# A fused attention and MLP kernel: the first loads on two queues, MLP columns and the weight transposes reordered in the opening

## The chip, the cores and the metric

One core of a Trainium2 chip runs the whole program. The metric is the time of one execution on the device, in microseconds (us). Engines are named as the profile names them: PE (matrix engine), PEld (its weight loads), DVE (VectorE), ACT (ScalarE), POOL (GpSimd), SP (the engine that issues most of the transfers here).

## The reference

The input is 2,048 tokens of 640 elements. The reference normalises them (LayerNorm without scale), puts the result through a linear attention of 32 heads with a softmax feature map and through a SwiGLU MLP of 1,536 columns, and adds both to the input. Everything is bf16. Cut to what matters here:

```python
xn = layernorm(x)
qkv = xn @ wqkv                                # 32 heads of 20
pk = einsum("bhsd,hdf->bhsf", k, w_phi)        # likewise pq from q
phi_k = concat([softmax(pk), softmax(-pk)])
o  = (phi_q @ (phi_k^T v)) / (phi_q . sum(phi_k) + 1e-6)
h  = silu(xn @ w1) * (xn @ w3)
out = x + o @ wo + h @ w2
```

## The kernel before

The kernel brings x in as sixteen tiles of 128 tokens. It needs xn transposed (`xnT`: channels on the partitions). Tiles 0 to 3 are transposed on PE; tiles 4 to 15 by DMA transposes, issued on the SP queue. Because `w_phi` is block diagonal, the kernel multiplies it into wk and wq once ("fold": `Wkp = wk @ blockdiag(w_phi)`), and for that it loads wk transposed (`wqkT`, five DMA transposes).

A list scheduler in the kernel file runs at build time. It models the engines and fixes a static order of instructions for each; waits follow from dependencies. All matmuls are issued by one helper and all vector work by another, so the profile shows one line number for each (L572 and L580 before, L619 and L627 after); the tiles' names tell them apart.

The loads, in the order of their priority:

```python
load_x(0, 1, lv)
load_x(1, 2, lv - 1)
load_wv(0, 2, lv - 2, "SP")
load_x(2, 3, lv - 3)
load_wv(2, 5, 2e9, "ACT")
load_x(3, 4, lv - 4)
load(phi_s[:], phi_t, 2e9 - 1e3, "ACT")
for e in range(DC):
    load_wT(1, e, lv - 9 - e)                  # wk, transposed by DMA
load_w13(0, 256, lv - 16)                      # MLP columns 0-255 of w1 and w3
load_x(4, 8, 1.9e6, "ACT")                     # held back by the model to 9 us
load_w13(256, 512, lv - 20)
load_x(8, 12, lv - 21)
load_w13(512, 1024, lv - 22)
load_x(12, 16, lv - 23)
load_w13(1024, 1536, lv - 24)
...
for t in range(4, T, 2):
    ln_stats(t, 2, 1e5 - t)
    ln_apply(t, 2e5 - t)
    ln_apply(t + 1, 2e5 - t)
    turn(xnT[:, :, t * 128:(t + 1) * 128], x_tok[:, t, :], lv)      # DMA transpose, on SP
    turn(xnT[:, :, t * 128 + 128:(t + 2) * 128], x_tok[:, t + 1, :], lv)
```

V of the first tiles does not wait for the whole LayerNorm: x is centred (by ACT and DVE, `CENTRED`), transposed and multiplied, and the scale is applied when V leaves PSUM. The full normalisation of the same tile, which K and the MLP need, is done apart; `POOLED` puts it on POOL for tiles 0 and 1:

```python
CENTRED = {0: "ACT", 1: "ACT", 2: "DVE", 3: "DVE"}
POOLED = (0, 1)
...
def ln_apply(t, level):
    o, m, s, z = x_tok[:, t, :], mv[:, t, 0:1], mv[:, t, 4:5], mv[:, t, 6:7]
    ways = [w_op("DVE", "tensor_scalar", (o, o, m, s, ALU.subtract, ALU.mult), 0.35, 0.44)]
    if t in POOLED:
        ways = [w_op("POOL", "tensor_scalar", (o, o, m, s, ALU.subtract, ALU.mult), 1.25, 1.3)]
    ...
```

V of tile 4 reads `xnT` and `wv`:

```python
def proj(t, w):
    for i in range(DC):
        for q in range(2):
            mm(q, lambda k, q=q: bank(k + q, 320), xnT[:, i, t * 128:(t + 1) * 128],
               w[:, i, 320 * q:320 * q + 320], i == 0, i == DC - 1)

def v_tile(t, level):
    P.begin(2, level, stream="V").name = f"V{t}"
    proj(t, wv)
    ...
```

One MLP column (`M0.0` is the first column of the first 512 tokens) is ten matmuls of 128x512, which PE issues every 0.216 us (215 or 216 ns between starts in the trace of before): about 2.16 us. The sums below use 2.155. These columns are what the scheduler puts wherever PE would otherwise wait.

The softmax here doesn't subtract the row's maximum and nothing guards it: scores larger than these inputs give would overflow.

## Time and profile before

| before | |
|---|---|
| time | 276.63 us, median of 4 runs, 276.57 to 276.64 |
| span in the profile | 274.9 us |
| first V matmul | 6.85 us |
| fold of wk starts | 15.78 us |
| first MLP column (M0.0) starts | 23.26 us |
| V of tile 4 starts | 33.84 us |
| `xnT` of tile 4 has landed | 29.68 us, so 4.16 us ahead of its use |

The first part of the profile's page has the busy time of each engine with its share of the span and its instructions; the second has the same in 40 slices of 6.9 us, in tenths. Before:

```profile
PE 266.7 (97%) x2078; PEld 158.9 (58%) x2097; DVE 183.1 (67%) x319; ACT 102.6 (37%) x187; POOL 65.7 (24%) x103
...
PE   6799999999999999999999999999999999999996
```

PE is the limit, and full from the third slice on. Only the opening has anything to give. What held it there is in the chain of waits (start, duration in us, what), followed back from what ended last in the first 41 us; its first microseconds, before:

```profile
0.81 2.27 DMA x_tok<-in_A_x_dram
...
5.74 2.53 POOL x_tok L580
...
9.36 2.53 POOL x_tok L580
...
11.93 0.45 PE PS L787 x5
```

Two normalisations of 2.53 us on POOL stand in line ahead of PE's transposes at 11.93 us. The scheduler's model had priced each at 1.25 to 1.3 us (the `ways` of `POOLED` above), half of what it took. The timeline of PE gives the order of its work (start, us from first start to last end, what, count; in brackets an idle time and what ended it). Before:

```profile
11.93 0.45 PE L787 MATMUL PS<-ident,x_tok 128*128 128x128 bf16 x5 [1.64 <-POOL x_tok L580]
...
15.78 1.87 PE L572 MATMUL PS<-BDc,wqkT 128*128 128x140 bf16 x30
17.60 5.61 PE L572 MATMUL PS<-Wkp,xnT 128*128 128x320 bf16 x40
23.26 10.74 PE L572 MATMUL PS<-xnT,w_s 128*128 128x512 bf16 x49
33.84 1.52 PE L572 MATMUL PS<-wv,xnT 128*128 128x320 bf16 x10
```

The rows after the POOL wait are the fold (`BDc,wqkT`), K of tiles 0 to 3 (`Wkp,xnT`) and five MLP columns (`xnT,w_s`; 49 of the 50 matmuls have a record). V of tile 4 (`wv,xnT`) follows at 33.84 us.

### The profile page before, as it was taken

The page shows a single profiled execution, that of the slowest core. Times are in us where ns is not written, and L with a number is a line of the kernel's source. Part 1 is how long each engine was busy: PE and PEld are TensorE (multiplying, and loading weights), DVE is VectorE, ACT ScalarE, POOL GpSimd, SP SyncE. Part 2 cuts the span into 40 slices and gives each one's busy share as a digit, 9 for nine tenths or more (in the row PEclk, how much of TensorE's full clock was granted, in tenths as well). Part 3 has the DMA queues.
Part 4 walks back from the last instruction along what each step waited for, and adds up shares of the span by engine and source line. Part 5 has one row for each costly group of instructions (what it writes and reads, how often), then busy time and mean ns, then how long its engine had stood idle before and what let it go on. Part 6 is the DMA issues. An engine that isn't in the chain of part 4 may idle for free.

```text
span 274.9 us, 5053 instructions
## 1 busy us (share of the span) xinstructions
PE 266.7 (97%) x2078; PEld 158.9 (58%) x2097; DVE 183.1 (67%) x319; ACT 102.6 (37%) x187; POOL 65.7 (24%) x103
## 2 busy tenths in 40 slices
PE   6799999999999999999999999999999999999996
PEld 3575477656654447544444445677777774444774
DVE  4698989999957433678978978577661215666112
ACT  6379377564553451256673382010000002222000
POOL 5923556999997000000000000000000000000000
PEclk9999999999999999999999999999999999999999
DMA  7999997910000000803211111243332222000001
GB/s 216 237 317 347 195 132 129 187 67 0 2 0 2 0 0 2 284 6 27 47 26 24 38 36 24 75 99 95 97 96 75 72 72 74 0 0 0 26 24 48
DMA packets 41255, 21.98 MB, mean 80 GB/s; under 512 B 27024, under 2 KB 41232, under 8 KB 41232
## 3 DMA queue, kind: packets, MB, share of 16 engines
q1 hardware_dynamic: 39648, 20.49, 31.2%
q10 hardware_dynamic: 1584, 1.17, 1.5%
q8 instruction: 16, 0.26, 0.4%
q14 instruction: 7, 0.06, 0.1%
HBM read 12.81 MB, written 2.62 MB: 56 GB/s over the span
## 4 chain that ended last, share of the span: by engine, by line
PE 91%; POOL 3%; ACT 2%; DVE 1%; issue 1%; DMA 1%
PE PS L572 91%; POOL x_tok L580 2%; ACT EqT L580 2%; DMA x_tok<-in_A_x_dram 1%; POOL mv L580 1%; PE PS L787 0%; DVE bst L580 0%; DVE hT L580 0%; DVE den_s L580 0%; DVE xres L580 0%; ACT e_s L580 0%; DVE xc L580 0%; PE PS L757 0%; DVE t L580 0%; DVE pr_s L580 0%
## 5 line engine op out<-in xcount | busy, mean ns | idle before, releaser
L572 PE MATMUL PS<-xnT,w_s 128*128 128x512 bf16 x465 | 105.6, 379 | 1.4 <-issue 0.5
L572 PEld LDWEIGHTS PS<-xnT,w_s 128*128 128x128 bf16 x480 | 46.4, 98 | 54.5 <-DVE hT L580 0.8
L572 PE MATMUL PS<-w_s,hT 128*128 128x320 bf16 x384 | 55.0, 299 | 0.0
L580 ACT ACTIVATE th<-PS 128x512 f32<-128x512 f32 x48 | 28.7, 599 | 66.0 <-PE PS L572 66.0
L580 DVE SCALAR_TENSOR_TENSOR t<-th,PS 128x512 bf16<-128x512 f32 x48 | 32.6, 679 | 24.0 <-ACT th L580 23.9
L572 PEld LDWEIGHTS PS<-w_s,hT 128*128 128x128 bf16 x384 | 37.1, 98 | 14.9
L580 DVE TENSOR_TENSOR xres<-PS,xres 128x640 bf16<-128x640 f32 (+1 forms) x17 | 13.4, 786 | 41.2 <-PE PS L572 41.2
L580 POOL TENSOR_TENSOR ekt<-ekt,rS 128x640 bf16<-128x640 bf16 x32 | 39.6, 1275 | 1.5 <-DVE rS L580 1.5
L580 DVE SCALAR_TENSOR_TENSOR hT<-t,PS 128x512 bf16<-128x512 bf16 x48 | 32.5, 677 | 1.3 <-PE PS L572 0.3
L580 ACT ACTIVATE EqT<-PS 128x512 bf16<-128x512 f32 x40 | 21.9, 594 | 12.6 <-PE PS L572 12.6
L580 DVE TENSOR_REDUCE S<-ekt 128x64 f32<-128x1280 bf16 x16 | 22.9, 1458 | 3.4 <-ACT ekt L580 3.4
L572 PE MATMUL PS<-wo_s,oT 128*128 128x320 bf16 x160 | 24.5, 299 | 0.0
L580 DVE TENSOR_TENSOR prod<-PS,g_s 128x1280 bf16<-128x1280 f32 x16 | 23.8, 1490 | 0.5
L580 ACT ACTIVATE ekt<-PS 128x640 bf16<-128x640 f32 x32 | 20.8, 701 | 8.6 <-PE PS L572 8.4
L572 PE MATMUL PS<-Wkp,xnT 128*128 128x320 bf16 x160 | 23.9, 299 | 0.0
L572 PE MATMUL PS<-xnT,Wqp 128*128 128x512 bf16 x96 | 23.1, 380 | 0.3 <-issue 0.2
L580 ACT ACTIVATE e_s<-PS 128x64 f32<-128x64 f32 x32 | 9.1, 284 | 37.6 <-PE PS L572 37.1
L572 PEld LDWEIGHTS PS<-wo_s,oT 128*128 128x128 bf16 x160 | 15.7, 98 | 6.1
L572 PEld LDWEIGHTS PS<-Wkp,xnT 128*128 128x128 bf16 x160 | 15.5, 98 | 6.0
L572 PE MATMUL PS<-wv,xnT 128*128 128x320 bf16 x120 | 18.3, 299 | 0.0
L580 DVE BATCH_NORM_STATS2 bst<-x_tok 128x6 f32<-128x320 bf16 x32 | 14.3, 469 | 3.0 <-DMA x_tok<-in_A_x_dram 3.0
L572 PEld LDWEIGHTS PS<-xnT,Wqp 128*128 128x128 bf16 x100 | 9.3, 98 | 10.8
(68 smaller groups left out, 172.1 us busy)
## 6 DMA issues: line engine op xcount, KB each, us to landing
w_s<-in_B_w_dram SPq DMA_DIRECT2D x4, 640.0 KB, 9.2
xres<-in_A_x_dram SPq DMA_DIRECT2D x16, 160.0 KB, 2.2
out_dram<-xres SPq DMA_DIRECT2D x15, 160.0 KB, 1.8
w_s<-in_B_w_dram SPq DMA_DIRECT2D x1, 1920.0 KB, 9.2
w_s<-in_B_w_dram SPq DMA_DIRECT2D x4, 320.0 KB, 5.5
x_tok<-in_A_x_dram SPq DMA_DIRECT2D x2, 640.0 KB, 8.4
wo_s<-in_A_wo_dram SPq DMA_DIRECT2D x1, 800.0 KB, 4.9
x_tok<-in_A_x_dram SPq DMA_DIRECT2D x4, 160.0 KB, 4.0
```

Of the source, the lines that this page charges most:

```text
L572: return nc.tensor.matmul(o(u.k), l, r, start=start, stop=stop, skip_group_check=shared)
L580: return getattr(e, name)(*[at(a, u) for a in args], **{k: at(v, u) for k, v in kw.items()})
```

## The change

Its intent is to start PE's real work earlier and to keep it fed. The first 1.5 MB alternate between the SP and the ACT queue; the normalisation of tiles 0 and 1 goes from POOL to DVE, and the mean of tile 2 for its centring from DVE to ACT; V of tiles 0 and 1 becomes one unit; w1 and w3 columns 0 to 383 are loaded early and three MLP columns stand ahead of the fold; and to let those loads through, the wk transposes wait until `w_phi` has landed. All later loads wait until the last wk transpose has landed (`d.raw.add(o)`). The scheduler's model of the DMA queues is rewritten and a new random seed chosen, with the random choices going on to 175 us of the model instead of 25; the first four loads of `xres` (x again, for the sum at the end) are held back to 60 us of the model. The core of the diff:

```diff
-CENTRED = {0: "ACT", 1: "ACT", 2: "DVE", 3: "DVE"}
-POOLED = (0, 1)
-SEED = 0
+CENTRED = {0: "ACT", 1: "ACT", 2: "ACT", 3: "DVE"}
+POOLED = ()
+SEED = 65
... (the model of the queues in the scheduler left out)
+    def v_pair(t, level):          # V of tiles t and t + 1 as one unit of four banks
+        P.begin(4, level, stream="V").name = f"V{t}+"
+        for a, b, u in ((0, 3, 0), (0, 3, 1), (3, DC, 0), (3, DC, 1)):
... (matmuls and copies as in v_first)
     load_x(0, 1, lv)
-    load_x(1, 2, lv - 1)
-    load_wv(0, 2, lv - 2, "SP")
-    load_x(2, 3, lv - 3)
-    load_wv(2, 5, 2e9, "ACT")
-    load_x(3, 4, lv - 4)
-    load(phi_s[:], phi_t, 2e9 - 1e3, "ACT")
+    on_act(1.3, load_x, 1, 2)
+    load_wv(0, 2, lv - 1)
+    on_act(1.75, load_wv, 2, 3)
+    load_x(2, 3, lv - 2)
+    on_act(2.2, load_wv, 3, 4)
+    load_wv(4, 5, lv - 3)
+    on_act(2.65, load_x, 3, 4)
+    load_w13(0, 384, lv - 4)
+    load(phi_s[:], phi_t, lv - 5)
+    first = [P.all[-1]]
     for e in range(DC):
-        load_wT(1, e, lv - 9 - e)
-    load_w13(0, 256, lv - 16)
+        o = load_wT(1, e, lv - 9 - e, first)
+    load_x(4, 8, lv - 19, "SP", [o])
     n = len(P.all)
-    load_x(4, 8, 1.9e6, "ACT")
-    late(n, 9.0)
-    load_w13(256, 512, lv - 20)
+    load_w13(384, 768, lv - 20)
     load_x(8, 12, lv - 21)
-    load_w13(512, 1024, lv - 22)
+    load_w13(768, 1152, lv - 22)
     load_x(12, 16, lv - 23)
-    load_w13(1024, 1536, lv - 24)
+    load_w13(1152, 1536, lv - 24)
     for e in range(DC):
         load_wT(0, e, lv - 30 - e)
+    for d in P.all[n:]:
+        d.raw.add(o)
...
-    for t in range(4):
+    v_pair(0, 6e4)
+    for t in range(2, 4):
         (v_first if t in CENTRED else v_tile)(t, 6e4 - 10 * t)
...
-    P.schedule({"PE": 1.25, "ACT": 2.1, "DVE": 0.93, "POOL": 0.8, "SP": 0.81}, filler, 12.0, SEED, 25.0)
+    P.schedule({"PE": 1.25, "ACT": 1.12, "DVE": 0.93, "POOL": 0.8, "SP": 0.81}, filler, 12.0, SEED, 175.0)
```

More of the change, by code (lines that the diff above doesn't have):

```diff
@@ L36 @@
     __slots__ = ("ways", "eng", "emit", "raw", "war", "bankd", "succ", "unit", "ismm", "start", "end", "inc", "sem",
-                 "clock", "idx", "part", "level", "off", "done", "nbytes", "busy", "left", "name", "deps", "gates", "early", "extra")
+                 "clock", "idx", "part", "level", "off", "done", "nbytes", "busy", "left", "name", "deps", "gates", "early", "extra",
+                 "begin", "each")
     def __init__(self, ways):
@@ L160, in op, with dma @@
         return self.add(o, writes, reads, level, after)
-    def dma(self, eng, emit, writes, reads, nbytes, busy=0.45, level=0.0, after=()):
+    def dma(self, eng, emit, writes, reads, pieces, each, busy=0.45, level=0.0, after=()):
         o = _Op({eng: (emit, busy, 0.0)})
-        o.nbytes = nbytes
+        o.nbytes, o.each = pieces, each
         return self.add(o, writes, reads, level, after)
@@ L206, in schedule @@
         bus = 0.0
+        issue = {"ACT": start["ACT"]}
+        queues = {"SP": [], "ACT": []}
         mode = "full"
@@ L215, in schedule, with transfer @@
                     ready[e].append(o)
+        def transfer(now):
+            nonlocal bus
+            at = dict.fromkeys(queues, 0)
+            left = {q: [o.nbytes for o in v] for q, v in queues.items()}
+            t = 0.0
+            bus = 0.0
+            while True:
+                go, wake = [], 1e9
+                for q, v in queues.items():
+                    if at[q] < len(v):
+                        o = v[at[q]]
+                        if o.begin <= t + 1e-9:
+                            go.append(q)
+                        else:
+                            wake = min(wake, o.begin)
+                if not go:
+                    if wake > 1e8:
+                        break
+                    t = wake
+                    continue
+                turn = sum(queues[q][at[q]].each for q in go)
+                steps = min(left[q][at[q]] for q in go)
+                if wake < t + steps * turn:
+                    steps = (wake - t) / turn
+                t += steps * turn
+                for q in go:
+                    left[q][at[q]] -= steps
+                    if left[q][at[q]] < 1e-6:
+                        o = queues[q][at[q]]
+                        e = t + 1.3 + o.extra
+                        if e > now:
+                            o.end = e
+                        at[q] += 1
+                bus = t
+            for q, v in queues.items():
+                while len(v) > 1 and v[0].end < now - 5.0 and v[1].begin < now - 5.0:
+                    v.pop(0)
         def commit(o, e, t):
-            nonlocal bus, pool_prev
+            nonlocal pool_prev
             o.eng = e
@@ L221, in commit @@
             o.start = t
-            free[e] = t + o.busy
+            free[e] = max(free[e], t + o.busy)
+            if e == "ACT":
+                issue[e] = t + (o.busy if o.nbytes else 0.06)
             if o.nbytes:
-                bus = max(bus, t + 0.6) + o.nbytes / 1e3
-                o.end = bus + 1.2 + o.extra
+                o.begin, o.end = t + 0.6, 1e9
+                queues[e].append(o)
+                transfer(t)
             else:
@@ L326, in schedule @@
                     continue
-                ts = [(max(free[e], op_time(o, e)), o) for o in ready[e]]
+                ts = [(max(issue[e] if o.nbytes and e == "ACT" else free[e], op_time(o, e)), o) for o in ready[e]]
                 t = min(x[0] for x in ts)
@@ L446, in emit @@
         return lists
-CENTRED = {0: "ACT", 1: "ACT", 2: "DVE", 3: "DVE"}
-POOLED = (0, 1)
-SEED = 0
+CENTRED = {0: "ACT", 1: "ACT", 2: "ACT", 3: "DVE"}
+POOLED = ()
+TURNED = ()
+SEED = 65
 TRIPLES = ((0, 3, 0, 60), (3, 3, 60, 60), (6, 3, 120, 60), (9, 3, 180, 60), (12, 3, 240, 60), (13, 3, 300, 20))
@@ L633, in bass_parallel_sum__linear_kernel_hedgehog__glu_gated_swiglu__prompt_kernel, with pieces @@
     queue = {"SP": nc.sync, "ACT": nc.scalar}
-    def bus(o, elem):
+    def pieces(o, elem):
         n = 1
@@ L638, in bus, with turn @@
             n *= s
-        return n * 2 / elem / 16 * max(18.0, 10 + 0.0352 * elem) + 100.0
+        return n * 2 / elem / 16, max(18.5, 12 + 0.04 * elem) / 1e3
     def load(o, i, level=0.0, eng="SP", after=()):
-        return P.dma(eng, lambda: queue[eng].dma_start(o, i), sb(o), sb(i), bus(o, 2 * o.shape[-1]), 0.45, level,
+        return P.dma(eng, lambda: queue[eng].dma_start(o, i), sb(o), sb(i), *pieces(o, 2 * o.shape[-1]), 0.45, level,
                      after)
-    def turn(o, i, level=0.0, dram=False):
-        d = P.dma("SP", lambda: nc.sync.dma_start_transpose(o, i), sb(o), sb(i), bus(o, 256),
-                  1.31, level)
+    def turn(o, i, level=0.0, dram=False, after=()):
+        d = P.dma("SP", lambda: nc.sync.dma_start_transpose(o, i), sb(o), sb(i), *pieces(o, 256),
+                  1.31, level, after)
         d.extra = 1.0 if dram else 0.2
@@ L658, in bass_parallel_sum__linear_kernel_hedgehog__glu_gated_swiglu__prompt_kernel, with load_x, load_w1, load_w3 @@
     w3_t = B_w3.rearrange("(c p) f -> p c f", p=128)
-    def load_x(a, b, level, eng="SP"):
-        load(x_tok[:, a:b, :], x_t[:, a:b, :], level, eng)
-    def load_w13(a, b, level, eng="SP"):
-        load(w1_s[:, :, a:b], w1_t[:, :, a:b], level, eng)
-        load(w3_s[:, :, a:b], w3_t[:, :, a:b], level, eng)
-    def load_wT(which, e, level):
-        turn(wqkT[:, which * DC + e:which * DC + e + 1, :],
-             A_wqkv[:, which * D + 128 * e:which * D + 128 * e + 128], level, True)
+    def load_x(a, b, level, eng="SP", after=()):
+        return load(x_tok[:, a:b, :], x_t[:, a:b, :], level, eng, after)
+    def load_w1(a, b, level, eng="SP"):
+        return load(w1_s[:, :, a:b], w1_t[:, :, a:b], level, eng)
+    def load_w3(a, b, level, eng="SP"):
+        return load(w3_s[:, :, a:b], w3_t[:, :, a:b], level, eng)
+    def load_w13(a, b, level, eng="SP"):
+        load_w1(a, b, level, eng)
+        load_w3(a, b, level, eng)
+    def load_wT(which, e, level, after=()):
+        return turn(wqkT[:, which * DC + e:which * DC + e + 1, :],
+                    A_wqkv[:, which * D + 128 * e:which * D + 128 * e + 128], level, True, after)
     zeroed = []
     def consts():
+        memset("DVE", warm[:], 0.0, 19)
         memset("DVE", zero[:], 0.0, 9)
         zeroed.append(P.all[-1])
-        memset("DVE", warm[:], 0.0, 9)
         add([w_act(warm[:], warm[:], ACT.Exp, 8)], [warm[:]], [warm[:]], None, 3e9)
@@ L730, in ln_apply @@
         if t in POOLED:
-            ways = [w_op("POOL", "tensor_scalar", (o, o, m, s, ALU.subtract, ALU.mult), 1.25, 1.3)]
+            ways = [w_op("POOL", "tensor_scalar", (o, o, m, s, ALU.subtract, ALU.mult), 2.5, 2.55)]
         if t >= 4:
@@ L777, in v_first, with src @@
             [v2[:, t, 0:672]], [r], [0, 1], 1e6)
+    def v_pair(t, level):
+        P.begin(4, level, stream="V").name = f"V{t}+"
+        for a, b, u in ((0, 3, 0), (0, 3, 1), (3, DC, 0), (3, DC, 1)):
+            for i in range(a, b):
+                for q in range(2):
+                    mm(2 * u + q, lambda k, q=q, u=u: bank(k + 2 * u + q, 320), xcT[:, t + u, i, :],
+                       wv[:, i, 320 * q:320 * q + 320], i == 0, i == DC - 1)
+            if b == DC:
+                o = v2[:, t + u, 0:672].rearrange("p (b h c) -> p b h c", b=2, c=21)[:, :, :, 0:DH]
+                r = mv[:, t + u, 4:5]
+                def src(k, u=u):
+                    return bank2(k + 2 * u, 320).rearrange("p b (h c) -> p b h c", c=DH)
+                add([w_act(o, src, ACT.Copy, D, r),
+                     w_op("DVE", "tensor_scalar", (o, src, r, None, ALU.mult), 0.74, 0.83)],
+                    [v2[:, t + u, 0:672]], [r], [2 * u, 2 * u + 1], 1e6)
     def xn_transpose(t, level):
@@ L1001, in out_tile @@
         load(xres[:, t % 4, :], x_t[:, t, :], 2e5 - 2 * t)
+        if t < 4:
+            P.all[-1].early = 60.0
         last = t == T - 1
@@ L1036, in bass_parallel_sum__linear_kernel_hedgehog__glu_gated_swiglu__prompt_kernel, with on_act, load_wv @@
     lv = 9e5
-    load_x(0, 1, lv)
-    load_x(1, 2, lv - 1)
-    def load_wv(a, b, level, eng):
-        load(wv[:, a:b, :], wqkv_t[:, a:b, 2 * D:3 * D], level, eng)
-    load_wv(0, 2, lv - 2, "SP")
-    load_x(2, 3, lv - 3)
-    load_wv(2, 5, 2e9, "ACT")
-    load_x(3, 4, lv - 4)
-    load(phi_s[:], phi_t, 2e9 - 1e3, "ACT")
+    def on_act(us, what, *args):
+        o = what(*args, 2e9, "ACT")
+        o.early = us
+        return o
+    def load_wv(a, b, level, eng="SP"):
+        load(wv[:, a:b, :], wqkv_t[:, a:b, 2 * D:3 * D], level, eng)
+        return P.all[-1]
+    load_x(0, 1, lv)
+    on_act(1.3, load_x, 1, 2)
[8 more added lines that the diff above has]
+    first = [P.all[-1]]
     for e in range(DC):
-        load_wT(1, e, lv - 9 - e)
-    load_w13(0, 256, lv - 16)
+        o = load_wT(1, e, lv - 9 - e, first)
+    load_x(4, 8, lv - 19, "SP", [o])
     n = len(P.all)
-    load_x(4, 8, 1.9e6, "ACT")
-    late(n, 9.0)
-    load_w13(256, 512, lv - 20)
+    load_w13(384, 768, lv - 20)
     load_x(8, 12, lv - 21)
-    load_w13(512, 1024, lv - 22)
+    load_w13(768, 1152, lv - 22)
     load_x(12, 16, lv - 23)
-    load_w13(1024, 1536, lv - 24)
+    load_w13(1152, 1536, lv - 24)
     for e in range(DC):
         load_wT(0, e, lv - 30 - e)
+    for d in P.all[n:]:
+        d.raw.add(o)
     up = 2e6
@@ L1074, in bass_parallel_sum__linear_kernel_hedgehog__glu_gated_swiglu__prompt_kernel @@
             xc_transpose(t, 6e4 - 10 * t + 15)
-        xn_transpose(t, 3e4 - t if t in CENTRED else 6e4 - 10 * t + 15)
+        if t in TURNED:
+            turn(xnT[:, :, t * 128:(t + 1) * 128], x_tok[:, t, :], 2e6)
+        else:
+            xn_transpose(t, 3e4 - t if t in CENTRED else 6e4 - 10 * t + 15)
     for t in range(4, T, 2):
```

## The prediction

> **What bounds it now.** TensorE. The page's busy table gives PE 97% of a 274.9 us span, the granted clock is full everywhere, and the chain of waits is 91% matmuls. The timeline of PE shows no gap above 0.3 us between 15.2 us and the end, so only the opening can give anything. The fold of wk starts at 15.78 us (timeline). Ahead of it lie four V tiles (2 x 2.88 us as displayed, about 5.5 us of issue) and eight sets of five transposes (about 0.28 us each, 2.2 us), some 7.7 us of real work: about 8 us of the opening is lost. The chain names its owner: x tile 0 lands at 3.08 us, statistics, then two normalisations of 2.53 us each on POOL (to 11.9 us), each ahead of the next tile's transposes. V starts at 6.85 us; its first wv piece lands at 6.72.
>
> **What changes.**
> 1. First loads alternate between the SP and ACT queues. By the Trainium skill, "DMA: Bandwidth & Descriptors", section on issuing engines, both feed the same 16 engines, so only issue time is saved (0.40 to 0.47 us per load here). The real effect is order: x tile 1 lands at about 3.7 instead of 4.26 us, the wv piece second on SP at about 5.5 instead of 6.72. V starts near 5.9 us, a microsecond earlier.
> 2. Normalising tiles 0 and 1 moves from POOL (2.53 us) to DVE (0.44 us). This removes about 4 us from the chain. But tile 2's centring goes to ACT (0.93 us), and DVE and ACT now carry it all: V copies of 0.8 us and transposes' copies of 0.5 to 0.7 us precede the last xnT piece. I expect PE gaps of some 1.5 us in 9 to 14 us; V and transposes end at about 14.2 us instead of 15.8.
> 3. The wk transposes wait for phi. Landings of before (293 to 350 GB/s) give an estimate of 7 to 7.5 us for the first 1.44 MB, 10.5 for 983 KB of MLP columns, 11 for phi. Five transposes at 1.27 us of issue and 3.6 us to landing: the last lands at about 20. Three MLP columns (6.5 us) fill that time; the fold starts at 20.1 to 20.8 us. The same work would have brought before there at 22.24, so the gain is 1.4 to 2.1 us.
> 4. Later loads start after the transposes, at about 20 us: x tiles 4 to 7 land near 24, and the first xnT transpose, behind 3.7 MB in the same queue, near 35.7 us. PE reaches V of tile 4 at about 36.2 (33.84 before, with two columns more ahead now). The slack is half a microsecond. After that PE is dense in both.
>
> PE work is the same.
>
> **Predicted: 275.1 us, 8 in 10 within 273.7 to 276.5** (276.63 before). Faster by over 2%: 0.02; within: 0.96; slower: 0.02.
>
> **Right if:** V starts near 5.9 us; the POOL normalisations leave the chain; the first MLP matmul starts at 13.5 to 14.5, the fold at 20 to 21, V of tile 4 at 35.5 to 37 us; PE dense afterwards.
>
> **Wrong if:** phi's 40-byte pieces or 768-byte rows load slowly, so that the fold waits; xnT of tile 4 comes after 37 us (the gain is lost there); the DVE chain of tiles 2 and 3 is longer than thought; or the new random seed of the list order places a stall in the PE-bound middle, where before has almost none to win back.

## The result, and the profile after

| | before | after |
|---|---|---|
| median of 4 runs each | 276.63 us | 277.15 us |
| range | 276.57 to 276.64 | 276.32 to 277.37 |
| ratio after / before | | 1.0014 (0.9993 to 1.0034, 95%) |
| span in the profile | 274.9 us | 275.7 us |

Ratios in this text are the mean time of one kernel's runs over the mean of the other's in the same rounds, so not quite the ratio of the medians quoted. The median lies outside the predicted range of 273.7 to 276.5, on the slow side. The changed kernel was run again without an edit: 276.64 (276.24 to 277.29), ratio 1.0001. The change moves the time by nothing that can be told from zero.

The page after:

```profile
PE 267.7 (97%) x2085; PEld 159.5 (58%) x2104; DVE 183.7 (67%) x322; ACT 102.8 (37%) x188; POOL 60.4 (22%) x101
...
PE   8999979999999999999999999999999999999996
```

The opening is fuller (8 and 9 where 6 and 7 stood), but the sixth slice, 34.5 to 41.3 us, has fallen from 9 to 7. The timeline of PE after says what stands there:

```profile
6.00 3.04 PE L619 MATMUL PS<-wv,xcT 128*128 128x320 bf16 x20
...
14.72 6.42 PE L619 MATMUL PS<-xnT,w_s 128*128 128x512 bf16 x29
20.98 1.86 PE L619 MATMUL PS<-BDc,wqkT 128*128 128x140 bf16 x30
22.88 5.61 PE L619 MATMUL PS<-Wkp,xnT 128*128 128x320 bf16 x40
28.54 8.58 PE L619 MATMUL PS<-xnT,w_s 128*128 128x512 bf16 x39
39.06 1.52 PE L619 MATMUL PS<-wv,xnT 128*128 128x320 bf16 x10 [1.94 <-DVE mv L627]
```

Three columns now lie ahead of the fold, four after K, and then PE waits 1.94 us for V of tile 4 (29 of 30 and 39 of 40 matmuls have a record). Before, no such wait existed. Note that the bracket names DVE.

How much did the opening give? Before started its fold at 15.78 us; with the same three columns (30 x 0.2155 = 6.47 us) ahead of it, it would have been 22.24. After: 20.98, so 1.26 us are gained. The POOL normalisations have left the chain, as the chain of waits of after over the same first 41 us shows:

```profile
2.35 6.08 DMA x_tok<-in_A_x_dram
...
8.87 0.37 DVE xc L627
...
9.64 0.36 DVE x_tok L627
...
10.83 1.36 PE PS L619 x10
```

The balance over the run, after minus before, from starts in the two timelines. Before is moved by the columns that the other has ahead of the same point: two columns (4.31 us) at V of tile 4, none at V of tile 15.

| stretch | us |
|---|---|
| up to the fold | -1.26 |
| fold to V of tile 4, without the wait | +0.23 |
| the wait ahead of V of tile 4 | +1.94 |
| V of tile 4 to V of tile 15 (79.58 against 78.24 us; 0.26 us of it is a wait for DVE that only after has) | +0.43 |
| from there to the end (the remainder; 0.3 us of it is a wait for DVE that only before has) | -0.63 |
| sum, the difference of the spans (275.65 - 274.94) | +0.71 |

The gain is real and is lost 18 us later, in one wait. Which engine does that wait belong to? Two views answer. First, the transfers in the order of the SP queue (timeline of SP; here the duration is that of the issuing, and a count over 1 joins several). After:

```profile
20.41 0.38 SPq L689 DMA_DIRECT2D x_tok<-in_A_x_dram  x1
20.84 1.08 SPq L689 DMA_DIRECT2D w_s<-in_B_w_dram  x2
21.95 0.53 SPq L689 DMA_DIRECT2D x_tok<-in_A_x_dram  x1
22.52 2.90 SPq L689 DMA_DIRECT2D w_s<-in_B_w_dram  x2
25.46 1.61 SPq L689 DMA_DIRECT2D x_tok<-in_A_x_dram  x1
27.12 1.45 SPq L689 DMA_DIRECT2D w_s<-in_B_w_dram  x1
28.95 9.56 SPq L693 DMA_TRANSPOSE xnT<-x_tok  x4
```

x tiles 4 to 7 are issued at 20.41, when the last wk transpose has landed. Then 3.77 MB of other loads go into the same queue, and only behind them the transposes of tiles 4 to 7. Before, x tiles 4 to 7 went out at 8.41 us on the ACT queue, and the transposes at 22.55:

```profile
22.55 7.64 SPq L646 DMA_TRANSPOSE xnT<-x_tok  x4
```

Second, the DMA view limited to the first of those transposes (the number is us from issue to landing). Before, issued at 22.55:

```profile
xnT<-x_tok SPq DMA_TRANSPOSE x1, 7.1
```

After, issued at 28.95:

```profile
xnT<-x_tok SPq DMA_TRANSPOSE x1, 10.0
```

So `xnT` of tile 4 landed at 29.68 before (V of tile 4 started 4.16 us later) and at 38.93 after (V of tile 4 started 0.13 us later). Landings after, from the trace, in queue order: x 4-7 at 24.59 us, w1 26.09, w3 27.69, x 8-11 29.52, w1 30.99, w3 34.13, x 12-15 35.83, w1 37.25, then `xnT` of tiles 4 to 7 at 38.93, 39.97, 40.56 and 41.15.

Against this stands the name in the bracket, "DVE mv". It is VectorE's mean-and-variance aggregate of a later x tile, which ended at 39.04 us. `v_tile` reads no `mv`. A bracket names what ended last by semaphore events shortly before the start; here that was a coincidence. But a reading is not a proof, and VectorE does free the PSUM banks that PE needs, so it stays as a rival for the experiments.

### The profile page after: what moved, and what is told of

It is laid out like the page before. It is cut to its first block, busy times and chain, and to the rows that moved or that the text cites. A ratio compares the mean times of both kernels' runs of the same rounds, so it can differ in the third digit from the quotient of the medians. Undisturbed runs are those within 1.5% of the kernel's fastest.

```text
span 275.7 us, 5062 instructions
## 1 busy us (share of the span) xinstructions
PE 267.7 (97%) x2085; PEld 159.5 (58%) x2104; DVE 183.7 (67%) x322; ACT 102.8 (37%) x188; POOL 60.4 (22%) x101
## 4 chain that ended last, share of the span: by engine, by line
PE 90%; DVE 4%; DMA 2%; issue 1%; ACT 1%; ACTq 0%; DVEq 0%
PE PS L619 89%; DMA x_tok<-in_A_x_dram 2%; DVE hT L627 1%; DVE t L627 1%; DVE prod L627 1%; DVE bst L627 0%; PE PS L857 0%; DVE den_s L627 0%; ACTq L689 0%; DVE Wqp L627 0%; ACT th L627 0%; ACT EqT L627 0%; ACT L627 0%; DVE xres L627 0%; ACT e_s L627 0%
## 5 line engine op out<-in xcount | busy, mean ns | idle before, releaser
L627 ACT ACTIVATE ekt<-PS 128x640 bf16<-128x640 f32 x32 | 20.8, 702 | 7.7 <-PE PS L619 7.5
L627 DVE BATCH_NORM_STATS2 bst<-x_tok 128x6 f32<-128x320 bf16 x32 | 14.2, 472 | 3.9 <-DMA x_tok<-in_A_x_dram 3.8
L619 PEld LDWEIGHTS PS<-wv,xnT 128*128 128x128 bf16 x120 | 11.7, 98 | 7.5 <-DVE mv L627 2.4
```

The lines of the kernel that those rows point to most:

```text
L619: return nc.tensor.matmul(o(u.k), l, r, start=start, stop=stop, skip_group_check=shared)
L627: return getattr(e, name)(*[at(a, u) for a in args], **{k: at(v, u) for k, v in kw.items()})
```

## The experiments

Theory A: the wait is for the landing of `xnT` of tile 4, which the backlog in the SP queue delays; take the backlog or the need away and the gain of the opening comes out whole. Theory B: the wait is for VectorE, which in the new order has more to do ahead of V of tile 4; reordering transfers does nothing.

Kernels e1 to e4 ran (before: 276.58 us, 276.46 to 277.27, 9 runs), e5 to e8 on another chip (before: 276.57, 276.48 to 276.94, 11 runs). All outputs were correct.

| run | median (range), us | ratio to before (95%) | fold | V of tile 4 | wait there | `xnT` of 4 landed |
|---|---|---|---|---|---|---|
| before | 276.63 | 1 | 15.78 | 33.84 | none | 29.68 |
| after | 277.15 (276.32-277.37) | 1.0014 (0.9993-1.0034) | 20.98 | 39.06 | 1.94 | 38.93 |
| e1, two loads behind the transposes | 275.18 (274.81-275.56) | 0.9948 (0.9936-0.9961) | 21.28 | 37.26 | none | 34.33 |
| e2, two more columns ahead of V 4 | 274.84 (274.70-275.43) | 0.9941 (0.9928-0.9954) | 20.57 | 40.87 | none | 38.31 |
| e3, wk transposes not gated | 275.21 (274.76-275.62) | 0.9946 (0.9934-0.9959) | 20.90 | 36.89 | none | 34.82 |
| e4, before with the norm on DVE | 276.32 (276.25-276.78) | 0.9991 (0.9978-1.0005) | 15.14 | 31.34 | none | 29.59 |
| e5, after again | 276.64 (276.24-277.29) | 1.0001 (0.9989-1.0013) | 20.73 | 38.29 | 1.42 | 38.16 |
| e6, before with the new first loads | 278.02 (277.69-279.38) | 1.0064 (1.0045-1.0084) | 18.38 | 34.41 | none | 30.24 |
| e7, e6 and e4 together | 276.50 (276.13-276.73) | 0.9994 (0.9982-1.0006) | 14.50 | 30.73 | none | 30.53 |
| e8, e2 and another VectorE order | 274.76 (274.63-275.05) | 0.9934 (0.9921-0.9947) | 20.76 | 41.06 | none | 38.17 |

Starts are us of the profiled run. e4, e6 and e7 have one column fewer ahead of V of tile 4 than before.

### e1: two late loads moved behind the transposes

The load of x tiles 12 to 15 and of w1's last columns (1.15 MB) are put behind the transposes of tiles 4 to 7 in the SP queue. The order of every compute engine stays as it was.

```diff
     load_x(12, 16, lv - 23)
+    held = [P.all[-1]]
     load_w13(1152, 1536, lv - 24)
+    held.append(P.all[-2])                     # w1 of columns 1152-1535
...
         turn(xnT[:, :, t * 128 + 128:(t + 2) * 128], x_tok[:, t + 1, :], lv)
+        if t == 6:
+            turn7 = P.all[-1]
...                                             (after the schedule is made)
+    for d in held:
+        P.ops.remove(d)
+    at7 = P.ops.index(turn7) + 1
+    P.ops[at7:at7] = held
```

> Only the order in SP's queue differs from the changed kernel: the load of x tiles 12 to 15 and one MLP load of 491 KB stand behind the four xnT transposes of tiles 4 to 7 instead of ahead of them. Theory A (the transposes stand in the queue behind loads nobody needs yet): the two loads took 1.70 and 1.42 us in the changed kernel, so xnT of tile 4 lands at about 35.8 instead of 38.93 us, PE gets there at 37.1, its wait of 1.94 us goes, and the time is about 275.2 us (0.995 of before). Theory B (the wait is on the statistics of VectorE, as the wait table names it): no compute engine's order is changed, so the wait stays at 1.5 to 2 us and the time at 277.1 (1.001).

Measured: 275.18 us, ratio 0.9948. The first transpose now lands 5.2 us after its issue (DMA view limited to it and the next two):

```profile
xnT<-x_tok SPq DMA_TRANSPOSE x3, 5.2
```

It landed at 34.33, and PE goes from its columns into V of tile 4 without a bracket:

```profile
28.84 8.58 PE L619 MATMUL PS<-xnT,w_s 128*128 128x512 bf16 x39
37.26 1.52 PE L619 MATMUL PS<-wv,xnT 128*128 128x320 bf16 x10
```

VectorE's and PE's orders were not touched, so theory B gives no reason for this. The trace says it more directly: the same aggregate of VectorE (38.83 to 39.04 us in after) ran from 39.13 to 39.34 us here, and V of tile 4 had started 1.87 us before it. The wait was for the transfer. The fold of this run was 0.30 us later than in after (its first loads came a little later: x tile 2 landed at 7.55 against 6.45 us), and still it was almost 2 us faster.

### e2: the loads left, the need put later

V and K of tile 4 may not start before MLP column 8 is done; the transfers stay as they are.

```diff
+    named = {u.name: u for u in P.units}
+    named["V4"].mms[0].war.add(named["M0.8"].mms[-1])
+    named["K4"].mms[0].war.add(named["M0.8"].mms[-1])
     P.schedule({"PE": 1.25, "ACT": 1.12, ...
```

> V and K of tile 4 are made to stand behind two more MLP columns on PE (their weights had landed at 34.1 us). Theory A: PE reaches V of tile 4 at about 41.4 us, after its xnT has landed (38.9), so the wait of 1.94 us goes and the time is about 275.2 us (0.995 of before). If instead the opening gained nothing and the slow part is elsewhere, the time stays at 276.6 to 277.4.

Measured: 274.84 us, ratio 0.9941. The transpose landed as late as in after, at 38.31 us. PE had six columns between K and V of tile 4 instead of four:

```profile
28.14 12.90 PE L619 MATMUL PS<-xnT,w_s 128*128 128x512 bf16 x58
40.87 1.52 PE L619 MATMUL PS<-wv,xnT 128*128 128x320 bf16 x10
```

Here the late landing costs nothing, because it comes 2.56 us before its use. Moved by the four columns more than before has ahead of it (8.62 us), V of tile 4 of before would start at 42.46, so 1.59 us are ahead: the opening's gain has come through. One caution: the scheduler also rearranged later work a little, so e1 is the cleaner proof that the transfer was the cause.

### e3: the wk transposes not held for w_phi

After the schedule was made, the dependency of the five wk transposes on the landing of `w_phi` was dropped; the orders stay.

```diff
+    gated = []
     for e in range(DC):
         o = load_wT(1, e, lv - 9 - e, first)
+        gated.append(o)
...                                             (after the schedule is made)
+    for d in gated:
+        d.raw.discard(first[0])
```

> The wk transposes no longer wait for phi; every order is as in the changed kernel. Theory A: they are issued from about 4.5 us, land by 15 instead of 20.40 us, x tiles 4 to 7 land near 19, xnT of tile 4 near 33, and the wait on PE goes: about 275.2 us (0.995). The fold stays at 20.98 us, since three MLP columns stand ahead of it. Rival (the gate is what makes the opening short, by keeping the transposes away from the first loads): the first MLP matmul comes more than 0.5 us later than 14.72 us and the time is 275.8 or more.

Measured: 275.21 us, ratio 0.9946. The wk transposes landed from 12.07 to 17.61 us (after: 15.81 to 20.40), x tiles 4 to 7 at 21.80 (24.59) and `xnT` of tile 4 at 34.82 (each later than expected, but early enough), 2.07 us ahead of its use:

```profile
28.47 8.58 PE L619 MATMUL PS<-xnT,w_s 128*128 128x512 bf16 x39
36.89 1.52 PE L619 MATMUL PS<-wv,xnT 128*128 128x320 bf16 x10
```

The gate is thus one place where the lateness was made: it pushes the wk transposes, these push every later load. It bought nothing in this run: the first MLP matmul on record started at 14.64 us and the fold at 20.90, as in after (14.72 and 20.98), although V started at 6.63 instead of 6.00.

### e4: only the normalisation off POOL

Before, with `CENTRED` and `POOLED` of the change and nothing else (so the mean of tile 2 goes to ACT too).

```diff
-CENTRED = {0: "ACT", 1: "ACT", 2: "DVE", 3: "DVE"}
-POOLED = (0, 1)
+CENTRED = {0: "ACT", 1: "ACT", 2: "ACT", 3: "DVE"}
+POOLED = ()
```

> The kernel before with one part of the change alone: tiles 0 and 1 are normalised on VectorE and tile 2 is centred on ScalarE; loads and gates as before. Theory A (the opening's gain is the 2 x 2.53 us of POOL that leave the chain, not the order of the loads): the fold starts near 14.3 instead of 15.78 us and the time is about 275.2 us (0.995). Rival (the order of the loads gives the gain): the fold starts at 15.3 us or later, and the time is 276.1 or more.

Measured: 276.32 us, ratio 0.9991, not to be told from before; the 275.2 of theory A was missed. The fold started at 15.14 us instead of the expected 14.3, and one set of transposes now follows it, so the gain is 0.36 us. The chain of waits of this run, followed back from 16 us, shows who is next in line:

```profile
2.20 5.15 DMA x_tok<-in_A_x_dram
...
8.29 0.40 DVE xc L580
```

x tile 2, the fourth load on the SP queue, lands at 7.34 us and then holds V of tiles 1 and 2. A chain of 5 us of POOL work was taken away and another, of the loads, stood 0.4 us behind it.

### e5: the changed kernel again

No edit.

> The changed kernel, not edited, beside the others. Theory A: again 276.3 to 277.4 us (1.000 to 1.003 of before), with one wait of 1 to 2 us on PE ahead of V of tile 4 that ends within 0.2 us of the landing of its xnT transpose, and the fold at 20.6 to 21.3 us.

Measured: 276.64 us, ratio 1.0001. The waits of PE (engine, its tile, what it waited for: total us, times, longest) of this run:

```profile
PE PS L619 <- DMA xnT<-x_tok: 1.4, 1, 1.4
```

It is the same wait, 0.5 us shorter, with V of tile 4 again 0.13 us behind the landing (38.29 and 38.16 us). This time the aggregate on VectorE did not end in that tenth of a microsecond, and the profile names the transfer. Two runs of one kernel, two names: a releaser's name is a hint.

### e6 and e7: which part made the opening faster

e6 gives before the new first loads alone; e7 adds the edit of e4.

```diff
-    load_x(1, 2, lv - 1)
+    on_act(1.3, load_x, 1, 2)
-    load_wv(0, 2, lv - 2, "SP")
-    load_x(2, 3, lv - 3)
-    load_wv(2, 5, 2e9, "ACT")
-    load_x(3, 4, lv - 4)
-    load(phi_s[:], phi_t, 2e9 - 1e3, "ACT")
+    load_wv(0, 2, lv - 1)
+    on_act(1.75, load_wv, 2, 3)
+    load_x(2, 3, lv - 2)
+    on_act(2.2, load_wv, 3, 4)
+    load_wv(4, 5, lv - 3)
+    on_act(2.65, load_x, 3, 4)
+    load(phi_s[:], phi_t, lv - 5)
...
-    P.schedule({"PE": 1.25, "ACT": 2.1, ...
+    P.schedule({"PE": 1.25, "ACT": 1.12, ...
```

> The kernel before with the order of its first loads alone changed (x tile 1 and wv pieces alternate between the queues, phi moves to SP). Theory C (two things hold up the opening of before: the landing of the first wv piece and the normalisations on POOL, and each hides the other): V starts at 6.0 to 6.4 instead of 6.85 us, but the second POOL normalisation still ends near 11.9 us and BDc, behind it on POOL, near 15, so the fold starts at 15.0 us or later and the time is 275.9 to 276.4 us. Rival (the load order is the whole gain): fold at 14.6 or earlier, 275.4 us or less.

Measured: 278.02 us, ratio 1.0064: slower, against the expectation, and the fold came at 18.38 us. V started 0.59 us earlier than before, but the second POOL normalisation still ended at 12.45 us, and PE sat idle for it and for what followed it. Then something else came in. The windows of this run (start:end, length, busy time of each engine with its instructions, granted clock, DMA share, GB/s):

```profile
core 0: us, PE busy (x) PEld busy (x) DVE busy (x) ACT busy (x) POOL busy (x), PEclk, DMA share, GB/s
12.00:15.50 3.50, 1.57 (x22) 1.07 (x21) 1.65 (x4) 1.35 (x2) 3.50 (x9) 0.99 1.13 317
15.50:18.40 2.90, 2.90 (x16) 1.69 (x14) 0.94 (x3) 0.15 (x1) 0.41 (x2) 0.50 1.16 296
```

PE was busy for 1.57 of 3.5 us, and afterwards it was granted half the clock, by the trace's clock record for 3.41 us (15.46 to 18.87; the second row lies inside). Ten V matmuls took 2.87 us in place of 1.52. The Trainium skill, "TensorE: Matmul & The Clock Gate", Part 1, says that the clock falls to half after about 3.4 us of idling. This trace shows the half clock, but PE had no idle stretch of 3.4 us here; the longest before it was 1.53 us (12.37 to 13.89). Two of the six runs (279.38, 279.37 us) have a mean clock of 0.994 and are over a microsecond slower than the other four (277.69 to 278.14, clock about 1.0). The profiled run is one of the two, so its fold is not that of the typical run; what made the other four slow (by about 1.3 us against before, 1.0047 by the means) has no trace.

> The kernel before with both the new order of its first loads and the normalisations on VectorE, but without MLP columns first, without the gate and without the later start of x tiles 4 to 7. Theory C: the two together give what neither gives alone: fold at 14.3 to 14.8 us (the wk transposes land near 14), V of tile 4 without a wait, and 275.1 to 275.6 us (0.995 to 0.9965). If the MLP columns in front are what the gain needs, the fold stays at 15.1 or later and the time at 276 or more.

Measured: 276.50 us, ratio 0.9994. The opening did as expected: the fold at 14.50 us with one set of transposes behind it, a gain of about 1.0 us, and V of tile 4 is 0.95 us ahead (30.73 + 2.155 = 32.88 against 33.84). The time did not follow. One loss is visible in the timeline:

```profile
44.99 2.11 PE L572 MATMUL PS<-xnT,w_s 128*128 128x512 bf16 x9 [0.48 <-ACT v L580]
```

A V copy on ACT freed a PSUM bank late. At V of tile 15 the run was still 0.48 us ahead and at the end 0.37 us; its own time was 276.30 us, and the other four lay between 276.13 and 276.73. `xnT` of tile 4 came only 0.20 us ahead of its use here, so the runs without a trace may have waited for it; that is not shown. These two kernels are not clean parts of the change, since the scheduler rearranges what follows; at the fold of the profiled runs the gains are -2.6 us (the loads, in a run at half clock) and +0.36 (the normalisation) alone, and +1.0 together. That speaks for the pair at the fold; in the time, e7 (276.50) is no better than e4 (276.32).

### e8: one step further

e2, with four VectorE operations of the opening moved ahead of others, to free the centred tile 2 earlier.

```diff
+    dve = [o for o in P.ops if o.eng == "DVE"]
+    for n, ahead in ((15, 14), (17, 14), (19, 18), (20, 18)):
+        P.ops.remove(dve[n])
+        P.ops.insert(P.ops.index(dve[ahead]), dve[n])
```

> The version with V of tile 4 behind two more MLP columns (274.84 us), and on VectorE the centring of tile 2 and the normalisation of tile 0 ahead of the statistics of tile 3, and the centring of tile 3 ahead of V's copy. In the changed kernel VectorE sat 0.86 us waiting for x tile 3 (to 8.46 us) while the sum for tile 2 was ready at 7.63. Expected: cT of tile 2 at 8.9 instead of 9.29 us, first MLP column at 13.8 to 14.2 instead of 14.3 to 14.7, fold at 20.0 to 20.5 (then held by the landing of the wk transposes), no wait ahead of V of tile 4, and 274.3 to 274.7 us (0.992 to 0.9935). If VectorE's order did not matter: 274.8.

Measured: 274.76 us, ratio 0.9934; e2 has 0.9941, so the step brought nothing that can be told, and the expectation was missed (first MLP matmul on record at 14.50 us, fold at 20.76). Centred tile 2 was ready at 8.23 us, but ScalarE's copy of V (8.86 to 9.66) now stood ahead of its copy of the transposed tile (9.68 to 10.38), and V of tile 2 started at 10.44. From the first V matmul to the first MLP column it took 8.17 us, against 8.22 in e2.

e2 and e8 are the fastest versions: both beat the kernel before and the changed one by 0.6 to 0.8%.

## Why the prediction was wrong

Point by point, prediction against the first run after:

| step | predicted | measured |
|---|---|---|
| 1. x tile 1, first wv piece, first V | 3.7, 5.5, 5.9 us | 3.61, 5.43, 6.00 us |
| 2. V and transposes done | 14.2 us | about 14.5 us |
| 3. first 1.44 MB, phi, last wk transpose, fold | 7-7.5, 11, 20, 20.1-20.8 us | 8.43, 11.34, 20.40, 20.98 us |
| 4. x tiles 4-7 | 24 us | 24.59 us |
| 4. PE reaches V of tile 4 | 36.2 us | 37.1 us |
| 4. `xnT` of tile 4 lands | 35.7 us | 38.93 us (again: 38.16) |
| time | 275.1 us | 277.15 us (again: 276.64) |

**Steps 1 to 3 were right in mechanism and nearly in size**, the first 1.44 MB excepted (1,440 KB of 1,024 bytes, so 1.47 MB as the other figures here count), which took a microsecond longer than estimated. The gain at the fold was 1.26 us, just under the predicted 1.4 to 2.1; the other runs with this opening had 1.52 (e5), 1.67 (e2), 1.34 (e3) and 0.96 (e1). Two queues gave no bandwidth: the Trainium skill, "DMA: Bandwidth & Descriptors", section "Issuing engines are not separate DMA queues", says that only issue time is saved, and the trace agrees as far as it goes: the same 1.47 MB had landed by 8.43 us with the queues in alternation, and by 7.77 us before, where ACT issued 0.49 MB of them. No run put all of them on one queue.

**Step 4 failed**: "the first xnT transpose, behind 3.7 MB in the same queue, near 35.7 us ... The slack is half a microsecond." It landed 3.2 us later. PE was 0.9 us later too, so the slack of 0.5 became a wait of 1.94. The prediction saw the danger and wrote it under "Wrong if" ("xnT of tile 4 comes after 37 us (the gain is lost there)"), but gave it too little weight for a slack of that size in a sum of eight transfers. The 11.7 us that it allowed from the landing of x tiles 4 to 7 to that of the transpose measured 14.34. The term splits as follows:

- x tiles 4 to 7 landed 0.6 us late.
- The 3.77 MB behind them took 12.66 us. One load of them, w3's columns 768 to 1151, took 3.14 us from the landing before it to its own, where loads of the same size took 1.4 to 1.6. In that time a packet of 16,384 bytes of the instruction queue took 1179 ns on one of the 16 DMA engines (at 31.91 us). Each of the ten traces (before, after, e1 to e8) has one such packet of 1.07 to 1.19 us amid its backlog of loads, and in each the load in flight took 2.4 to 3.2 us from the landing before it (before: 3.21 us, packet at 19.66; e3: 2.43 us, packet at 31.19). The Trainium skill, "Runtime: NRT & Kernel Launch", section "Instruction fetch mechanics", says that instructions are refilled in blocks of 16 KiB through a DMA queue of their own; the trace agrees (16 packets, 0.26 MB). Packet and slow load coincide in time in every trace; whether one causes the other no run tested.
- The first transpose landed 1.68 us behind the last load, where later ones followed each other at 0.59 to 1.04 us. Ahead of it the transfers nearly stood still, as the windows of after show (columns as in the windows of e6):

```profile
35.50:37.00 1.50, 1.50 (x8) 0.54 (x6) 1.14 (x4) 0.60 (x1) 0.56 (x4) 1.00 0.14 22
37.00:39.00 2.00, 0.12 (x1) 0.00 (x0) 1.97 (x6) 0.00 (x0) 0.00 (x0) 1.00 1.29 134
```

From 35.5 to 37.0 us the DMA share is 0.14, at 22 GB/s, a fifteenth of the 331 GB/s from 33.0 to 35.2, while w1's last load had still to land and two transposes had been issued. In these 1.5 us only 35 of the loads' packets of 768 bytes start, where there had been about 100 in a quarter of a microsecond; packets of 256 bytes, the transposes' size, had begun at 34.69, and the last ones begun before the stop took 1.6 to 2.0 us and ended together at 37.1. I take it that one lagging engine finished its share of the load while the transposes, begun on the others, stood until then; this is an inference. This stop lies ahead of w1's landing (37.25), so it belongs to the 12.66 us, and before, e1 and e3 have one like it (12 to 33 GB/s for 1.0 to 1.2 us).

The 1.68 us themselves hold a second stop: 31 GB/s from 37.50 to 38.25 us. After the last load's landing e2, e5 and e8 have one too (7 to 9 GB/s for 0.55 to 0.60 us), and their first transpose came 1.52 to 1.66 us behind that load; the other six traces have none there, and it came 0.57 to 0.74 us behind. What makes the second stop is not known. A packet of 8,192 bytes of the other instruction queue took 1993 ns in the first stop (at 35.44); in e2 and e5 the same packet took 0.34 to 0.35 us and the first transpose still came 1.66 us behind the last load, so that one was not needed for it. The second row above is the lost time itself: PE busy for 0.12 of 2 us.

With the wait gone, by three different means, the time is 275.18 (e1), 274.84 (e2) and 275.21 us (e3), around the predicted 275.1. That agrees with the rest of the prediction, and it confirms theory A. Theory B falls with e1, where no compute engine's order changed and V of tile 4 started before the aggregate that the bracket had named; the repeat, where the same wait bears the transfer's name, fits.

**What stays open**: whether the instruction fetch causes the slow load; what causes the second stop ahead of the first transpose; how the gain of the opening divides between the pairing of V and the MLP columns ahead; what the new seed by itself did to the later stretches (+0.43 and -0.63 us in the balance), since no run has the change with the old one; and why e7 kept so little of its gain in the median, and four runs of e6 were so slow.

## What to carry to other kernels

When loads are pushed later to help the opening, follow the whole queue to its first consumer: the slack of the last thing behind the backlog decides whether the gain survives, and half a microsecond of slack behind 3.8 MB is none, since here one slow load cost 1.5 us and the first transpose another microsecond. Put what PE needs next ahead of what it needs later in the same queue, or give PE work that needs nothing from it; either recovered the gain here, 0.5 to 0.6%. And before acting on the engine that a wait's bracket names, check that the waiting instruction reads anything of it, and look at a second run.

## What the Trainium skill lacked or had wrong

- "Runtime: NRT & Kernel Launch", section "Instruction fetch mechanics", calls the cost of a block boundary mostly hidden. It does not say what the refill may do to other transfers: packets of 16,384 bytes took 1.07 to 1.19 us on one DMA engine here, and the loads in flight landed 2.4 to 3.2 us behind the load before, where others of their sizes in the backlog took 1.1 to 1.9. The cause is not proven, but a page that plans transfers needs the number.
- "DMA: Bandwidth & Descriptors" has the effective bandwidth of a DMA transpose (261 GB/s where the middle dimension is not contiguous, section "Latency and other measured facts"; by it 160 KB take an estimated 0.63 us, and before's second to fourth transposes landed 0.59, 0.73 and 0.64 us apart, so these agree; after's landed 1.04, 0.59 and 0.59 apart). It lacks what the first transpose behind a backlog of loads takes: 0.57 to 0.74 us after the last load in six traces, 1.52 to 1.68 us in four.
- "TensorE: Matmul & The Clock Gate", Part 1, ties the fall of the clock in its table to an idle window of about 3.4 us; further down it tells of another kernel whose frequent short idle times brought the fall too, but gives no measure of how busy PE may be when it comes. In e6 the clock was halved for 3.41 us after a stretch in which PE was busy for 1.57 of 3.5 us and never idle for longer than 1.53 us at a time, in two of six runs by their mean clock.
- No page warns that a profile's releaser can be a coincidence: the same wait bore the name of VectorE in one run (1.94 us) and of the transfer in another (1.42 us).
